# A state-space layer with an MLP on one core: the written-out order of 1078 operations is searched anew

## The chip, the core and the metric

One core of a Trainium2 chip. The metric is device microseconds for one execution of the whole program; the kernel before and the kernel after are run on the same kind of core and compared. In the profile the engines are called PE (TensorE, matmuls; PEld its weight loads), DVE (VectorE), ACT (ScalarE), POOL (GpSimd) and SP (SyncE, which here only issues DMAs).

## The reference

The input u has 2048 steps of 512 channels (bf16). It is normalized, sent through a diagonal state-space layer (a long convolution whose kernel K is built from 128 complex exponentials for each channel), added to itself, normalized twice more, and sent through an MLP with 1376 hidden units. Cut to what matters:

```python
def _A_ref(u, A_re, A_im, B_re, B_im, C_re, C_im, log_dt, Dskip):
    dt = jnp.exp(log_dt)[:, None]
    logdA, dB = dt * (A_re + 1j * A_im), dt * (B_re + 1j * B_im)
    l = jnp.arange(L).astype(A_re.dtype)                     # bf16
    P = jnp.exp(logdA[:, :, None] * l[None, None, :])
    K = jnp.einsum("dn,dnl,dn->dl", C_re + 1j * C_im, P, dB).real
    ...                                                      # both padded to 2 L
    Yf = rfft2(up) * rfft2(Kp)
    y = irfft2(Yf)[..., :L]
    return y.transpose(0, 2, 1) + u * Dskip

def _B_ref(x, w1, b1, w2, b2):
    h = gelu(einsum("bsd,df->bsf", layernorm(x), w1) + b1)
    return einsum("bsf,fd->bsd", h, w2) + b2

h = x + _A_ref(layernorm(x), ...)
return h + _B_ref(layernorm(h), w1, b1, w2, b2)
```

## The kernel before

The program first makes a list of 1078 operations, each with the engines that it may run on, a cost for each, and what it reads and writes. Then `Sched.run` walks through `ORDER`, a list written out by hand: a value k stands for operation `k // 2`, and `k % 2` picks the first or the second of its allowed engines. A cost is used for three things only: a planned start of each operation, the merging of the engines by that start, and the placing of fills. On one engine the operations are issued in the order of the list, so costs alone do not reorder an engine. The core of it:

```python
for k in ORDER:
    i, e = k // 2, ops[k // 2].eng[k % 2]
    s = max(free[e], ready(ops[i], e), ...)
    ...
    if e == "PE" and s > FILL0 and s - free[e] > 0.6 and fs:
        ...   # dummy matmuls of 512 columns up to s, through Sched.fill (line 1443)
order.sort(key=lambda o: (o.start, o.i))
```

A fill is such a dummy matmul: it stands on PE where the plan sees PE waiting for over 0.6 us, and its result is not used. Matmul results go to four PSUM buffers of 128x1024 floats. An eviction copies such a buffer to the arena in SBUF (the tile `ar`), on ScalarE (line 554) or VectorE (line 556) as the list says. Most DMAs go through SP's queue, in the order of the list; log_dt, C_re and B_re are issued by ScalarE, ahead of its work. The convolution is done as a two-step Fourier transform of 64 by 32 points, with the matrices of cosines and sines made on the chip. The stages, with the names that the prediction uses:

- *Loads and tables.* The parameters are transposed on PE. dt is an Exp (ScalarE). The angles of A_im are wrapped and restacked by 16 small DMAs on SP. GpSimd makes constants, among them the weights W2 for the chains (line 718) and a mask block: `R_fn` (lines 842 to 846) and its product with a one-hot row (a TT, line 612). From these it makes the masks W of the frequency matrices (line 602).
- *Statistics and normalizing of u.* Sixteen bn_stats (line 906) and, later, sixteen normalizing steps (line 915) on VectorE.
- *Exponentials.* `bexps` (line 767) are sixteen Exp steps on ScalarE; `aexps` (matmuls at 983, 987) five for each half of the channels.
- *Chains.* `chain(half, kind)` builds the powers of the complex exponentials, as B0, A0, B1 and A1. For each group of four powers PE adds a phase in PSUM (line 1029), ScalarE takes two sines (line 1037) and VectorE multiplies (lines 1055 to 1057, for A1 1042 and 1043).
- *Transforms of u.* `austage` (line 928) regroups u into AU_d in DRAM, X0 and X1 are read back by SP, and `xspec`/`fstage` (line 954) transforms them. X0 and X1 are the two halves of the sequence.
- *Kernel chunks.* `kgen` (lines 1079, 1080; chunks 0 and 1) and `kgen4` (1110, 1111; chunks 2 and 3) contract the powers over the 128 states. After each chunk one VectorE step (line 1093, or 1120) adds Dskip to its first tap; the prediction calls it the correction. `kspec` (line 1144) is the first step of the chunks' transform; its result makes a round trip through AK_d in DRAM, and `fstage` does the second step.
- *Inverses.* `inverse(b, c)` for half b and chunk c: products of spectra on VectorE (line 1184), 96 or 192 small matmuls (line 1194), an eviction, and on SP a transposing DMA (the "transpose" of an inverse, line 1200).
- *Tails.* `tail(b, sb)`: matmuls (line 1274) that put the halves together and, for the first tail, add u; bn_stats and, but for the first, an addition ahead of it (lines 1281, 1282); a Newton iteration of small VectorE steps for the inverse root; four normalizing steps (VectorE at 1297 or ScalarE at 1299); and a transpose, on PE for the first tail (line 1307), by DMA for the others. The Gelu table is loaded once, on ScalarE.
- *MLP.* `mlp(b, sb)` four times: matmuls at line 1328, Gelu on ScalarE (1330), matmuls at line 1350, an addition on VectorE (1352), two DMAs out.

Of the kernel before, what the change touches and what calls it, by code (L numbers as in the profile page):

```python
# [154 lines left out]
class VS(V):  # L155
# [260 lines left out]
def c_act(n, ptr=0):  # L416
    return 0.055 + n / 1200.0 + 0.09 * min(ptr, 1)
# [7 lines left out]
def kernel(ctx, tc, A_u, A_A_re, A_A_im, A_B_re, A_B_im, A_C_re, A_C_im, A_log_dt, A_Dskip,  # L425
# [125 lines left out]
    def evac(out_fn, in_fn, n, r, w, pr=None, only=None):  # L551
# [5 lines left out]
        if only == "ACT":  # L557
            add("ACT", c_act(n), fn, r=r, w=w, pr=pr)
        elif only == "DVE":
            add("DVE", c_dve(n, 1, True), fn, r=r, w=w, pr=pr, hv=0)  # L560
        else:
            add(("ACT", "DVE"), (c_act(n), c_dve(n, 1, True)), fn, r=r, w=w, pr=pr)
# [925 lines left out]
```

## Time and profile before

| | |
|---|---|
| three runs | 262.06, 262.65 and 264.29 us, median 262.65 |
| the profiled execution | 262.22 us, its span 260.4 us, mean granted clock of TensorE 0.991 |
| busy in the span | PE 226.0 us (87%), VectorE 185.7 (71%), ScalarE 172.0 (66%), GpSimd 50.2 (19%) |
| DMA | 34.34 MB, mean 132 GB/s |
| ScalarE's table of sines loaded | 37.26 to 38.54 us |
| first chain product, last A0 product, last A1 product | 51.7, 74.8, 105.3 us |
| first matmul of line 1144 | 95.9 us |
| first matmul of inverse (1,0) | 131.5 us |
| end of the last product of inverse (0,3) | 153.96 us |
| first matmul of the first tail, first matmul of the MLP | 161.6, 174.2 us |
| last matmul | 256.6 us |

The span runs from the first to the last recorded instruction; the 1.8 us to the execution's own time lie around it. The points in time in the lower half are how the prediction cuts the kernel into stages: each is the start or the end of a named group of instructions in the trace. A busy share of PE is not work alone, since fills count as matmuls (line 1443).

### The profile page before, as it was taken

The numbers are of one execution on the slowest core, as the hardware profiler recorded it, in microseconds if no ns is written. First come the engines' busy times: TensorE is split into PE (matmuls) and PEld (weight loads), VectorE is DVE, ScalarE is ACT, GpSimd is POOL, SyncE is SP. The second block draws the span as 40 slices with busy tenths as digits, with TensorE's granted clock in tenths as the row PEclk, the third lists the DMA queues.
The fourth block names the chain that finished last, engine by engine and source line by source line (L and its number), as shares of the span: only waits on it lengthen the run. The fifth ranks groups of instructions, "written<-read, shape, count | busy, mean of one in ns | idle before, by whom it ended". The sixth has DMA issues, their size and how long they took to land.

```text
span 260.4 us, 7255 instructions
## 1 busy us (share of the span) xinstructions
PE 226.0 (87%) x3019; PEld 130.7 (50%) x3032; DVE 185.7 (71%) x363; ACT 172.0 (66%) x207; POOL 50.2 (19%) x236
## 2 busy tenths in 40 slices
PE   7209995868698988999999999799999999989994
PEld 3105751423475654675578885464344444434542
DVE  3999999999998889666899996798585424021021
ACT  3989997958997569768996970757602913912710
POOL 8934442997028000000000000000000000000000
PEclk9999999997999999999999999999999999999999
DMA  6600011463584458679289899999341402050303
GB/s 203 262 0 3 3 45 35 124 117 89 121 279 130 128 149 297 219 215 331 90 239 255 227 179 200 265 168 252 81 85 25 94 7 49 18 99 23 88 5 76
DMA packets 46001, 34.34 MB, mean 132 GB/s; under 512 B 26161, under 2 KB 42386, under 8 KB 45970
## 3 DMA queue, kind: packets, MB, share of 16 engines
q1 hardware_dynamic: 45378, 33.44, 48.6%
q10 hardware_dynamic: 592, 0.46, 0.6%
q8 instruction: 23, 0.38, 0.6%
q14 instruction: 8, 0.07, 0.1%
HBM read 16.32 MB, written 10.49 MB: 103 GB/s over the span
## 4 chain that ended last, share of the span: by engine, by line
PE 59%; DVE 23%; ACT 8%; DMA 4%; issue 4%; POOL 0%; DVEq 0%; ACTq 0%; POOLq 0%
PE ps L1328 13%; PE ps L1350 13%; PE ps L1194 7%; PE ps L954 4%; DMA ar<-ar 4%; ACT ar L554 4%; PE ps L1144 4%; DVE ar L906 3%; PE ps L1029 3%; ACT ar L1037 3%; DVE ar L915 3%; DVE ar L1056 3%; DVE ar L612 3%; DVE ar L617 2%; PE ps L1274 2%
## 5 line engine op out<-in xcount | busy, mean ns | idle before, releaser
L554 ACT CAST ar<-ps 128x1024 bf16<-128x1024 f32 (+3 forms) x69 | 63.2, 983 | 20.2 <-DVE ar L1282 6.9
L1330 ACT ACTIVATE ar<-ps,ar 128x512 bf16<-128x512 f32 (+1 forms) x44 | 28.7, 686 | 40.4 <-PE ps L1328 27.0
L1352 DVE TENSOR_TENSOR ar<-ps,ar 128x512 bf16<-128x512 f32 (+1 forms) x17 | 11.0, 658 | 45.0 <-PE ps L1350 43.1
L1328 PE MATMUL ps<-ar 128*128 128x512 bf16 (+1 forms) x176 | 40.3, 379 | 1.0 <-DMA ar<-ar 0.7
L1037 ACT ACTIVATE ar<-ps 128x1024 bf16<-128x1024 int16 x36 | 34.9, 1044 | 8.0 <-DVE ar L1056 3.2
L1350 PE MATMUL ps<-ar 128*128 128x512 bf16 (+3 forms) x181 | 39.7, 366 | 0.3
L556 DVE CAST ar<-ps 128x1024 bf16<-128x1024 f32 (+4 forms) x31 | 32.7, 1070 | 8.0 <-PE ps L1111 3.6
L602 POOL TENSOR_SCALAR ar<-ar 128x128 bf16<-128x128 bf16 (+6 forms) x60 | 31.0, 540 | 18.6 <-ACT ar L624 18.1
L1184 DVE TENSOR_TENSOR ar<-ar 128x1024 bf16<-128x1024 bf16 x48 | 30.1, 685 | 3.3 <-PE ps L1194 2.0
L1328 PEld LDWEIGHTS <-ar 128*128 128x128 bf16 (+1 forms) x176 | 17.5, 100 | 22.2 <-issue 2.6
L1350 PEld LDWEIGHTS <-ar 128*128 128x128 bf16 (+1 forms) x187 | 18.1, 98 | 20.5 <-issue 1.1
L1029 PE MATMUL ps<-ar 128*32 128x256 f16 x560 | 22.0, 279 | 4.9 <-ACT ar L1037 4.4
L1194 PE MATMUL ps<-ar 64*128 64x128 bf16 x768 | 23.5, 216 | 1.8 <-DVE ar L1282 1.4
L1194 PEld LDWEIGHTS <-ar 64*128 64x128 bf16 x768 | 21.6, 94 | 5.3 <-issue 2.8
L1029 PEld LDWEIGHTS <-ar 128*32 128x32 f16 x560 | 13.8, 97 | 14.4 <-issue 14.1
L954 PE MATMUL ps<-ar 128*64 128x512 bf16 (+1 forms) x160 | 17.8, 342 | 0.7 <-DVE ar L556 0.4
L767 ACT ACTIVATE ar<-ar 128x1024 bf16<-128x1024 f32 x16 | 15.9, 1047 | 1.1 <-DVE ar L600 1.1
L1056 DVE TENSOR_TENSOR ar<-ar 128x1024 bf16<-128x1024 bf16 x21 | 16.1, 783 | 0.2
L983 PE MATMUL ps<-ar 128*128 128x512 f16 x24 | 7.4, 430 | 9.8 <-DVE ar L600 9.6
L1057 DVE TENSOR_TENSOR ar<-ar 128x1024 bf16<-128x1024 bf16 x21 | 14.0, 690 | 0.3
L624 ACT ACTIVATE ar<-ar 128x512 f32<-128x512 f32 (+8 forms) x18 | 11.7, 679 | 3.6 <-DMA ar<-in_A_log_dt_dram 2.7
L928 PE MATMUL ps<-ar 128*128 128x512 bf16 x26 | 8.7, 411 | 5.2 <-DVE ar L600 4.0
(99 smaller groups left out, 315.2 us busy)
## 6 DMA issues: line engine op xcount, KB each, us to landing
AU_d<-ar SPq DMA_DIRECT2D x16, 256.0 KB, 3.8
ar<-AU_d SPq DMA_DIRECT2D x8, 512.0 KB, 4.1
ar<-AK_d SPq DMA_DIRECT2D x8, 512.0 KB, 5.9
ar<-in_A_u_dram SPq DMA_DIRECT2D x4, 512.0 KB, 5.3
AK_d<-ar SPq DMA_DIRECT2D x2, 1024.0 KB, 4.4
ar<-in_A_u_dram SPq DMA_DIRECT2D x8, 256.0 KB, 4.7
AK_d<-ar SPq DMA_DIRECT2D x4, 512.0 KB, 3.6
out_dram<-ar SPq DMA_DIRECT2D x30, 64.0 KB, 2.0
```

What stands on the lines that cost most here:

```text
L554: act.copy(out_fn(), in_fn())
L556: dve.tensor_copy(out_fn(), in_fn())
L602: en.tensor_scalar(a, b, f(s1), f(s2), op0, op1)
L954: pe.matmul(pst(p)[64 * h:64 * h + 64, w * (k + r):w * (k + r) + w], lhsT=T.ap()[:, f, r, :], rhs=v[f:f + 1].ap()[:, 0, :], start=True, st ...
L1029: pe.matmul(pst(p)[32 * g:32 * g + 32, 256 * j:256 * j + 256], lhsT=W2[DELTAS.index(d)].ap(), rhs=S2[g].ap()[:, ch0:ch0 + 256], start=Fals ...
L1037: add("ACT", c_act(1024), lambda e, p=p, sc=sc, cs=cs: act.activation(swo(sc[cs]) if hf and kind == "B" else sc[cs].ap().rearrange("p a b ...
L1056: add("DVE", c_dve(1024, 2), lambda e, lo=lo, rv=rv, Sx=Sx, e0=e0, i0=i0, q=q: dve.tensor_tensor(ent(i0, q, lo, 4, rv), ent(e0, q, lo, 4, ...
L1184: dve.tensor_tensor(o, a, b_[:, :, ::-1, :] if sw else b_, ALU.mult)
L1194: pe.matmul(pst(p)[:, 512 * h + 128 * k:512 * h + 128 * k + 128], lhsT=q.ap()[rows, 2 * k + r, :], rhs=TP[w].ap()[rows, f0 // 2 + k, :], s ...
L1328: pe.matmul(pst(p)[:fs, 512 * z:512 * z + 512], lhsT=w1s[dc].ap()[:, fc * P:fc * P + fs], rhs=ybuf.ap().rearrange("p (t c) k -> p c t k", ...
L1330: add("ACT", c_act(512, 1), lambda e, p=p, z=z, fc=fc, fs=fs: act.activation(hT.ap()[:fs, fc, :], pst(p)[:fs, 512 * z:512 * z + 512], ACT. ...
L1350: pe.matmul(pst(p)[:, 512 * z + c0:512 * z + c1], lhsT=hT.ap()[:fs, fc, 128 * t:128 * t + 128], rhs=w2s[fc].ap()[:fs, c0:c1], start=(fc == ...
```

## The change

The computation, the buffers, the operations and the tiles stay as they are, and so do all line numbers. Two things are edited. The list `ORDER` is another permutation of the same 1078 operations, with another choice of engine for some; and the costs that the planner uses are changed for evictions, products, normalizing of u and most kinds of matmuls. Cut to its core (46 lines of numbers are replaced):

```diff
 ORDER = [
-    22, 28, 24, 82, 0, 358, 60, 30, 2, 4, 8, 114, 288, 112, 90, 188, 190, 32, 118, 6, 78, 72, 116, 122, 156, 134, 26, 286, 34, 36, 38, 272, 158, 160, 68,
...
+    288, 358, 306, 0, 4, 362, 24, 114, 2, 68, 8, 30, 76, 32, 34, 36, 38, 72, 22, 112, 156, 188, 190, 118, 116, 122, 128, 78, 152, 158, 26, 54, 64, 6, 120,
...
 ]
     def evac(...):
-            add("ACT", c_act(n), fn, r=r, w=w, pr=pr)
+            add("ACT", c_act(n) + (0.1 if n > 700 else 0), fn, r=r, w=w, pr=pr)
     def unorm(pr):
-            add("DVE", c_dve(512, 4) + 0.13, ufn, ...)
+            add("DVE", c_dve(512, 4) + 0.23, ufn, ...)
     def fstage(v, nb, soft=()):
-            add("PE", 0.86 if nb == 1 else 0.45, fn, ...)
+            add("PE", 0.99 if nb == 1 else 0.53, fn, ...)
     def aexps(pr):
-                add("PE", 1.75 if n < 3 else 0.88, fn, ...)
+                add("PE", 1.93 if n < 3 else 0.97, fn, ...)
     def chain(hf, kind, pr):
-                o = add("PE", 0.55 + (0 if gn else 0.45 if kind == "B" else 1.3), fn, ...)
+                o = add("PE", 0.58 + (0 if gn else 0.47 if kind == "B" else 1.36), fn, ...)
-                add("DVE", c_dve(1024, 2), ...)              # each of the four products
+                add("DVE", c_dve(1024, 2) + 0.08, ...)
     def kgen(c, pr):
-                    add("PE", 0.14 * (hi - lo), fn, ...)
+                    add("PE", 0.148 * (hi - lo), fn, ...)
     def kgen4(c, pr):
-                add("PE", 0.13 * h, fn, ...)
+                add("PE", 0.148 * h, fn, ...)
     def kspec(b, q, pr, ak, nb, n):
-                add("PE", 4 * len(vs) * (0.22 if par is None else 0.12), mm, ...)
+                add("PE", 4 * len(vs) * (0.255 if par is None else 0.14), mm, ...)
     def inverse(b, c, pairs, zt, pr):
-            add("PE", 0.47 * len(jobs), fn, ...)
+            add("PE", 0.479 * len(jobs), fn, ...)
     def tail(b, sb, ybuf, pr):
-            add("PE", 0.85 if first else 0.43 * (1 + b), fn, ...)
+            add("PE", 0.98 if first else 0.5 * (1 + b), fn, ...)
-                add("PE", 0.3, fn, ...)                      # transposes
+                add("PE", 0.33, fn, ...)
```

What the new list does, read from the order in which each engine is given its instructions:

- *Engines.* Of 104 evictions 72 were on ScalarE and 32 on VectorE; now 77 and 27. Of the tails' sixteen normalizing steps eight were on each; now ten are on ScalarE.
- *Fills* go from 49 to 38, and stand elsewhere: before, 16 behind the exponentials of A, 3 in chain B1, the rest beside the inverses (15 around inverse (1,2), 12 in inverse (1,3)); now 15 behind the exponentials, 11 beside inverse (1,2), 6 in inverse (1,3), and a few single ones.
- *DMA issues.* ScalarE issues C_re ahead of log_dt; SP issues A_im behind all four loads of u; SP's loads of w1 and x stand elsewhere between the transposes.
- *GpSimd.* The mask block and the constants of u's transform move behind the product for the angle of A (the TT of `gi`); W2 stays ahead of the chains.
- *PE.* The transforms of X0, which stood among the sines of A1, move for the most part behind the kernel chunks; the first half of inverse (1,0) goes ahead of inverse (0,0).
- *First tail.* Its small statistics steps, which had four products of an inverse between them, stand together; the Gelu table is loaded between its evictions.

More of the change, by code (lines that the diff above doesn't have):

```diff
@@ L561, in evac @@
         else:
-            add(("ACT", "DVE"), (c_act(n), c_dve(n, 1, True)), fn, r=r, w=w, pr=pr)
+            add(("ACT", "DVE"), (c_act(n) + (0.1 if n > 700 else 0), c_dve(n, 1, True)), fn, r=r, w=w, pr=pr)
     def dma(q, out_fn, in_fn, byts, r, w, pr=None, soft=(), k=1.0):
@@ L915, in ufn @@
                 dve.tensor_scalar(a, a, sc_, bi_, ALU.mult, ALU.add)
-            add("DVE", c_dve(512, 4) + 0.13, ufn, r=[x_sb[s], nw[3], nw[4]], w=[x_sb[s]], pr=pr + 0.001 * (s // 4))
+            add("DVE", c_dve(512, 4) + 0.23, ufn, r=[x_sb[s], nw[3], nw[4]], w=[x_sb[s]], pr=pr + 0.001 * (s // 4))
     def austage(b, pr, soft=()):
@@ L988, in aexps @@
                 S.pr = pr + 0.1 * n + 0.5 * hf
-                add("PE", 1.75 if n < 3 else 0.88, fn, r=[HLt] + [WA[LV.index(LD[4 * n + j])] for j in range(4)] + ([HLg, Ih] if n < 3 else []), w=[p], new=[p] if n < 3 else [], soft=[TBL])
+                add("PE", 1.93 if n < 3 else 0.97, fn, r=[HLt] + [WA[LV.index(LD[4 * n + j])] for j in range(4)] + ([HLg, Ih] if n < 3 else []), w=[p], new=[p] if n < 3 else [], soft=[TBL])
                 if hf == 0:
@@ L1080, in fn @@
                                 pe.matmul(o, lhsT=Ai.ap()[:, :, d], rhs=Bi.ap()[:, :, d], start=False, stop=True, tile_position=(0, 32 * g))
-                    add("PE", 0.14 * (hi - lo), fn, r=[Ar, Br, Ai, Bi], w=[p], new=[p] if first else [])
+                    add("PE", 0.148 * (hi - lo), fn, r=[Ar, Br, Ai, Bi], w=[p], new=[p] if first else [])
                     first = False
@@ L1111, in fn @@
                         pe.matmul(o, lhsT=w(Ai), rhs=x(Bi), start=False, stop=True)
-                add("PE", 0.13 * h, fn, r=[EA2, Br, IA2, Bi], w=[p], new=[p] if b == 0 else [])
+                add("PE", 0.148 * h, fn, r=[EA2, Br, IA2, Bi], w=[p], new=[p] if b == 0 else [])
             def ofn(j0=j0, h=h):
@@ L1144, in mm @@
                             pe.matmul(oo, lhsT=W[v].ap()[rows, tl, :], rhs=r, start=(m == 0), stop=(m == len(js) - 1), tile_position=(32 * g, 0))
-                add("PE", 4 * len(vs) * (0.22 if par is None else 0.12), mm, r=[kg, W], w=ps, new=ps if first else [])
+                add("PE", 4 * len(vs) * (0.255 if par is None else 0.14), mm, r=[kg, W], w=ps, new=ps if first else [])
                 first = False
@@ L1274, in fn @@
                             pe.matmul(o[64 * h:64 * h + 64], lhsT=DD.ap()[:, di].rearrange("p a b -> p (a b)"), rhs=rhs, start=(n == 0 and not first), stop=(n == len(terms) - 1))
-            add("PE", 0.85 if first else 0.43 * (1 + b), fn, r=[identb, DD] + [hs[8 * b + 4 * sb + 2 * jp + z] for z in range(2)] + ZT0 + (ZT1 if b else []), w=[p], new=[p])
+            add("PE", 0.98 if first else 0.5 * (1 + b), fn, r=[identb, DD] + [hs[8 * b + 4 * sb + 2 * jp + z] for z in range(2)] + ZT0 + (ZT1 if b else []), w=[p], new=[p])
             for z in range(2):
```

16 lines of the change are left out of this document (8 added, 8 removed), and 78 rows, old and new, of the table ORDER.

## The prediction

> **What bounds the kernel now.** I read the page, then the busy times in six stages that I cut at the starts of groups of matmuls, then the chain that ended last, then the groups by shape. The first two lines are the page, the others the stages: after the span come PE, weight loads, VectorE, ScalarE and GpSimd busy, the granted clock, the DMA share and GB/s.
>
> ```profile
> span 260.4 us, 7255 instructions
> ...
> PE 226.0 (87%) x3019; PEld 130.7 (50%) x3032; DVE 185.7 (71%) x363; ACT 172.0 (66%) x207; POOL 50.2 (19%) x236
> ...
> 41.60:75.00 33.40, 25.78 (x382) 12.56 (x391) 32.60 (x58) 28.16 (x31) 17.35 (x32) 0.95 0.49 124
> 75.00:104.00 29.00, 26.20 (x829) 17.74 (x833) 26.11 (x41) 22.08 (x26) 7.18 (x14) 1.00 0.57 183
> 104.00:131.50 27.50, 26.74 (x354) 17.16 (x344) 19.76 (x26) 23.15 (x26) 0.52 (x1) 1.00 0.66 213
> 131.50:157.60 26.10, 25.28 (x686) 21.09 (x686) 25.36 (x38) 20.60 (x22) 0.00 (x0) 1.00 0.92 228
> 157.60:174.20 16.60, 14.64 (x248) 9.24 (x249) 11.79 (x33) 7.17 (x10) 0.00 (x0) 1.00 1.10 213
> 174.20:256.60 82.40, 81.05 (x392) 37.18 (x396) 32.90 (x90) 34.95 (x53) 0.00 (x0) 1.00 0.31 71
> ```
>
> From 41.6 to 75 (chains B0 and A0) VectorE is full, 32.60 of 33.40, and PE waits. From 75 to 104 PE and VectorE are both near full. From 104 to 131.5 PE is. From 131.5 to 157.6 (the inverses) VectorE is full again, 25.36 of 26.10; PE's 25.28 holds fills. The last row, the MLP, is PE alone: 81.05 of 82.40. The row ahead of it is not work but a chain of latencies:
>
> ```profile
> 151.80 2.81 PE ps L1194 x96
> 154.68 0.86 ACT ar L554
> 155.59 1.03 ACT ar L554
> 156.63 4.96 DMA ar<-ar
> 161.63 0.41 PE ps L1274 x2
> ...
> 172.51 1.08 PE ps L1307 x16
> 173.61 1.02 ACT ar L554
> 174.68 7.93 PE ps L1328 x36
> ```
>
> The evictions of inverse (0,3) end, their transposing DMA takes 4.96 us, the tail's first matmul starts at once, and 13 us of statistics, normalizing and transposes follow until the MLP. So the run's end is the MLP's start plus some 82 us of matmuls.
>
> **The change, part by part.** Nothing is computed otherwise; 1078 operations stand in another order, and some move between ScalarE and VectorE. For both kernels I took the order of issue on each engine and summed, ahead of chosen instructions, the durations of the same form in this trace (for matmul groups, from the start of one to the start of the next). The sums differ from elapsed time by some per cent, as instructions overlap at their ends or wait, so I use differences, scaled by what the same stretch took before. The forms that move:
>
> ```profile
> L554 ACT CAST ar<-ps 128x1024 bf16<-128x1024 f32 x61 | 58.7, 1026 | 10.3 <-PE ps L1194 3.8 <-PE ps L954 3.1 <-PE ps L928 1.5
> L556 DVE CAST ar<-ps 128x1024 bf16<-128x1024 f32 x19 | 23.0, 1218 | 2.6 <-PE ps L954 1.7 <-PE ps L928 0.7
> L1299 ACT ACTIVATE ar<-ar 128x512 bf16<-128x512 bf16 x8 | 6.3, 807 | 3.5 <-DVE ar L617 3.5
> L1297 DVE TENSOR_SCALAR ar<-ar 128x512 bf16<-128x512 bf16 x8 | 3.0, 411 | 0.1
> ```
>
> *Engines.* Evictions on VectorE fall from 32 to 27 and rise on ScalarE from 72 to 77; normalizing steps go from 8 and 8 to 6 on VectorE and 10 on ScalarE. The net five are small: six of 264 to 792 columns leave VectorE, one more of 1024 comes to it. In sums VectorE loses 4.4 us and ScalarE gains 4.9. Fills fall from 49 to 38; at 0.216 us from start to start 11 are 2.4 us, but they stand where PE waited, so I don't add them.
>
> *To the start of L1144, 95.9: +0.1.* On ScalarE's queue log_dt is now issued behind C_re, 0.43 us later (issues stood at 0.77 and 1.20), and ScalarE, with 36.4 us of work ahead of its sine table in both, passes that on; but VectorE sets this stretch from 34 us. Its work up to the correction of the kernel's second chunk (L1093), the last step ahead of L1144, is 91.5 in both. In between it is moved: up to the last A0 product 2.0 us more (two evictions and a B1 product go ahead), from there 1.8 less. PE has 0.2 more ahead of L1144. Bounds: -1.3, the part of VectorE's work in 75 to 95.9 that would be saved if the A0 products weren't waited for (1.8, less 0.5); +4.7 by ScalarE, which has 4.3 us more ahead of the last eviction that L1144 needs, plus the 0.4. ScalarE idled 12.2 us in 41.6 to 104, so I take VectorE's value. A_im now follows all four loads of u on SP; its first user on VectorE stood at 21.97 us, 12 us after its transpose, and PE had nothing else until 19.5: free. GpSimd's mask block (L842 2.62 us, L612 2.16) moves behind the product for the angle; W2, which the first chain needs, still comes ahead of the restacked angles, which land at 44: free, up to 5 us; what it may do to VectorE is a rival.
>
> *95.9 to 131.5 (first matmul of inverse (1,0)): 0.* PE is full and has 29.1 us of work in both. VectorE's last A1 product comes 4.0 us of work sooner and the AK_d DMAs some 2 us sooner after L1144, but the X0 transforms (L954), which stood among the A1 sines, now stand here and PE does not finish earlier. Bounds: -2.6, PE's three longest gaps of 79 to 99 us (0.92, 0.93, 0.74); 0.
>
> *131.5 to the last product of inverse (0,3), 153.9: -0.8.* VectorE decides. Before, it ends the last eviction that the inverses need at 132.5 and has 22.9 us of work to that product, done in 21.4. After, the like eviction ends just as inverse (1,0) starts (+0.1), and 23.0 follow: 21.5. So 21.6 against 22.4. Bounds: -2.3, PE's count (19.8 to 17.5); 0. On SP, ahead of the transpose of (0,3), one 344 KB load of w1 is added and one 256 KB load of x goes: free.
>
> *From there to the MLP: -0.9.* The 4.96 us transpose stays. From the tail's first matmul to the MLP it was 13.4 us. Now the 15 small statistics steps stand together instead of with four 0.68 us products among them, but three normalizing steps are on ScalarE at 0.81 instead of 0.41, and the Gelu table (1.28) is loaded inside. Step by step: 1.5 to the first bn_stats, 4.0 for four of them and two products, 2.8 statistics, 2.4 normalizing, 0.3 transposes, 1.5 eviction and start: 12.5. Bounds: -2.4, the 11 fills with their waits; +1.3, the table load in full.
>
> *MLP: -0.7.* Same matmuls. Its one stall is 0.73 us at 231.8, for the transpose of the last tail, whose matmuls now stand 4.7 us of PE work sooner. The one ahead of it is issued later, behind the first MLP's output sums, with some 20 us of matmuls to cover it; without that cover, 4.7.
>
> Sum: 0.1 - 0.8 - 0.9 - 0.7 = -2.3. The profiled run took 262.2 (span 260.4 and 1.8 around it), 0.4 below the median of 262.65. Forecast **259.9**.
>
> **The rivals.**
> *ScalarE sets the pace (slower).* If its waits stay as they are, the work moved to it comes on top: +4.7 at L1144, the inverses -0.8, the tail +1.3 with the table load in full, the MLP -0.7: 266.7. For: ScalarE ran 81% from 41.6 to 104. Against: part of its idle time is VectorE's buffers, which come sooner:
>
> ```profile
> ACT ar L1037 <- DVE ar L1056: 3.2, 3, 2.0
> ```
>
> It decides once ScalarE is above some 95% there.
> *GpSimd holds VectorE up (slower).* Two L915 steps, 0.41 us each elsewhere, took 2.40 together while GpSimd ran two steps of 1.29:
>
> ```profile
> 38.41 2.40 DVE L915 TENSOR_SCALAR ar<-ar 128x512 bf16<-128x512 bf16 x2
> ```
>
> Such losses after 27 us were 1.6 here and 1.5 at one L602 (1.96 instead of 0.43). The moved block and what follows it last 2.62 + 2.16 + 1.19 + 1.29 + 1.29 = 8.6 us, now beside VectorE's sixteen L915. If all of it held VectorE, 8.6 - 3.1 = 5.5 more: 265.4. Against: the nine bn_stats (L906) beside two GpSimd steps at 24 us kept their 0.68 us each, so not every kind is held. [...]
> *The DMA hides it (no change).* The share is 0.92 and 1.10 ahead of the MLP. If the transposes land when they did, only tail and MLP are left: 260.7; if each engine waits for its producers as before, 262.2. Against: the transposes wait on SP for evictions.
> *More gain*, the full bounds of inverses, tail and MLP: 262.2 - 2.3 - 2.4 - 0.7 = 256.8, and with the gaps 254.2.
>
> **How the numbers follow.** Forecast 0.38 (its own range 257.8 to 261.5), more gain 0.18, no change 0.16, GpSimd 0.08, ScalarE 0.20. Run times differ by 0.9% here, so 1% is about what can be told. Below 260.0: more gain and 0.24 of the forecast's 0.38, as its own range reaches further below than above, 0.42. Above 265.3: ScalarE, and some of GpSimd's, 0.22. Within: 0.36. The range runs from 255.0, short of the fullest gain, to 266.7, ScalarE's price.
>
> **What would show it.** Right: the first L1144 within 1 us of 95.9, the first matmul of inverse (1,0) near 131.5, the MLP's first L1328 near 172.6, 27 evictions on VectorE, no stall in the MLP. Wrong: ScalarE above 95% from 41.6 to 104 with a late L1144; L915 above its mean of 0.51 us; a transpose of over 6 us ahead of the tail; an MLP of over 82.4 us. An L1144 ahead of 94 would show that counting VectorE's work misses waits that the list takes away.

## The result, and the profile after

The change made the kernel slower: 265.64 us (median of 20 executions, 262.84 to 267.50) against 263.74 us (20 executions, 262.06 to 266.76), a ratio of 1.0065 with a 95% interval of 1.0038 to 1.0092. The forecast was 259.9, which is 2.8 below the 262.65 that three executions of before gave; against all twenty the change is +1.9 by medians and +1.8 by means. Ratios with intervals leave out executions over 1.5% above the fastest of their kernel, which favours a kernel that scatters; medians and means are over all. `ORDER` holds 1079 operations, numbered 0 to 1078, so one more than the 1078 named above. The profiled execution of the kernel after took 265.12 us. The page:

```profile
span 263.3 us, 7270 instructions
...
PE 227.4 (86%) x3021; PEld 131.7 (50%) x3021; DVE 183.9 (70%) x356; ACT 176.9 (67%) x214; POOL 56.5 (21%) x236
...
PEclk9999979998999999999999999889999999999998
```

VectorE lost work and ScalarE gained it, as forecast, and PE has the same work. VectorE's busy time fell by 1.8 us only, not by the 4.4 that were counted; the steps that were held, below, fill the gap. What is new is GpSimd, 56.5 us busy instead of 50.2 for the same 236 instructions, and two more dips of PE's clock. The cut at the times used before shows that GpSimd's time was added from 41.6 to 75, where its mask steps (L602, 128x128) stand; columns as before:

```profile
41.60:75.00 33.40, 26.25 (x381) 12.37 (x381) 32.91 (x66) 29.40 (x34) 24.08 (x36) 0.95 0.49 129
75.00:104.00 29.00, 24.35 (x801) 17.09 (x793) 21.68 (x38) 23.08 (x28) 5.20 (x11) 1.00 0.50 153
...
157.60:174.20 16.60, 14.52 (x225) 9.22 (x221) 10.46 (x29) 9.28 (x12) 0.00 (x0) 0.90 1.08 195
174.20:256.60 82.40, 81.59 (x461) 37.95 (x458) 34.98 (x95) 37.15 (x56) 0.00 (x0) 1.00 0.36 77
```

The 24.08 us of GpSimd in the first row are not the loss: the first experiment below has 24.48 there and loses nothing. These rows have shifted against the work, so I cut both kernels again at the starts and ends of the same operations (us; the last column has two other profiles of the old order: the mask block later in the kernel before, and the old list with the new costs):

| stretch | before | after | old order again |
|---|---|---|---|
| to the first L928 | 41.6 | 44.7 | 41.6, 41.7 |
| to the first chain product (L1056) | 51.7 | 55.3 | 51.8, 51.8 |
| from there to the first matmul of inverse (1,0) | 79.8 | 78.9 | 80.2, 81.2 |
| to the last product of inverse (0,3) | 22.5 | 21.9 | 22.6, 22.9 |
| to the tail's first matmul that did not wait | 7.7 | 8.2 | 7.7, 7.7 |
| to the MLP's first that did not wait | 13.3 | 14.9 | 14.8, 14.8 |
| the MLP | 81.7 | 80.3 | 81.6, 80.8 |

The kernel after is 3.6 us late before the first product of the chains, gets 1.5 us back up to the inverses' last product, loses 2.1 around the tail and gains 1.4 in the MLP: 2.8 in all. The profile of before that I predicted from was a good one of its kind: its tail had the full clock and took 13.3 us, where the same order took 14.8 twice, at a clock of 0.88. A fourth profile of that order (codT and product elsewhere, below) had the full clock and 13.3 again.

### The profile page after: what moved, and what is told of

Its sections match the earlier page's. It is cut to its first block, busy times and chain, and to the rows that moved or that the text cites. A ratio compares the mean times of both kernels' runs of the same rounds, so it can differ in the third digit from the quotient of the medians.

```text
span 263.3 us, 7270 instructions
## 1 busy us (share of the span) xinstructions
PE 227.4 (86%) x3021; PEld 131.7 (50%) x3021; DVE 183.9 (70%) x356; ACT 176.9 (67%) x214; POOL 56.5 (21%) x236
## 4 chain that ended last, share of the span: by engine, by line
PE 56%; DVE 25%; ACT 9%; issue 5%; DMA 4%; ACTq 0%; DVEq 0%
PE ps L1328 15%; PE ps L1350 15%; PE ps L1194 6%; PE ps L954 5%; DVE ar L617 4%; ACT ar L1037 3%; DVE ar L906 3%; ACT ar L554 3%; PE ps L1144 3%; DVE ar L600 3%; DVE ar L612 3%; DVE ar L1056 2%; DMA ar<-ar 2%; PE ps L1029 2%; DVE ar L1057 2%
## 5 line engine op out<-in xcount | busy, mean ns | idle before, releaser
L554 ACT CAST ar<-ps 128x1024 bf16<-128x1024 f32 (+3 forms) x74 | 66.4, 959 | 18.8 <-PE ps L1274 5.2
L602 POOL TENSOR_SCALAR ar<-ar 128x128 bf16<-128x128 bf16 (+6 forms) x60 | 37.3, 642 | 9.4 <-DVE ar L602 7.9
L556 DVE CAST ar<-ps 128x1024 bf16<-128x1024 f32 (+3 forms) x26 | 29.2, 1140 | 9.6 <-PE ps L1111 3.1
L1184 DVE TENSOR_TENSOR ar<-ar 128x1024 bf16<-128x1024 bf16 x48 | 29.9, 685 | 5.5 <-PE ps L1194 5.4
L1328 PEld LDWEIGHTS <-ar 128*128 128x128 bf16 (+1 forms) x176 | 17.3, 100 | 20.7 <-issue 1.0
L1194 PE MATMUL ps<-ar 64*128 64x128 bf16 x768 | 25.2, 222 | 1.9 <-issue 1.3
L1194 PEld LDWEIGHTS <-ar 64*128 64x128 bf16 x768 | 22.9, 97 | 5.6 <-issue 4.1
L1029 PE MATMUL ps<-ar 128*32 128x256 f16 x560 | 20.9, 276 | 3.3 <-issue 1.9
L1029 PEld LDWEIGHTS <-ar 128*32 128x32 f16 x560 | 13.9, 97 | 11.9 <-issue 11.6
L954 PE MATMUL ps<-ar 128*64 128x512 bf16 (+1 forms) x160 | 17.0, 341 | 0.4 <-ACT ar L554 0.3
L983 PE MATMUL ps<-ar 128*128 128x512 f16 x24 | 8.0, 454 | 8.6 <-DVE ar L600 5.7
L617 DVE SCALAR_TENSOR_TENSOR ar<-ar 128x4 f32<-128x4 f32 (+5 forms) x44 | 14.4, 335 | 1.2 <-ACT ar L624 0.3
L1056 DVE TENSOR_TENSOR ar<-ar 128x1024 bf16<-128x1024 bf16 x21 | 14.4, 707 | 0.8 <-ACT ar L1037 0.7
L1057 DVE TENSOR_TENSOR ar<-ar 128x1024 bf16<-128x1024 bf16 x21 | 14.3, 716 | 0.3 <-ACT ar L1037 0.2
```

The costliest lines, as they stand in the source:

```text
L554: act.copy(out_fn(), in_fn())
L556: dve.tensor_copy(out_fn(), in_fn())
L602: en.tensor_scalar(a, b, f(s1), f(s2), op0, op1)
L617: add("DVE", c_dve(n, 1, psum), lambda e: dve.scalar_tensor_tensor(oap() if oap else o.ap(), aap() if aap else a.ap(), f(s), bap() if bap ...
L954: pe.matmul(pst(p)[64 * h:64 * h + 64, w * (k + r):w * (k + r) + w], lhsT=T.ap()[:, f, r, :], rhs=v[f:f + 1].ap()[:, 0, :], start=True, st ...
L1029: pe.matmul(pst(p)[32 * g:32 * g + 32, 256 * j:256 * j + 256], lhsT=W2[DELTAS.index(d)].ap(), rhs=S2[g].ap()[:, ch0:ch0 + 256], start=Fals ...
```

## What holds VectorE ahead of the chains

The answer to the first two rows lies at 28 to 38 us of the kernel after. The timeline of GpSimd, then of VectorE (start, us, instruction, shapes, count):

```profile
28.62 0.87 POOL L842 MEMSET ar<- 128x928 f32 x1
29.54 1.50 POOL L846 MEMSET ar<- 128x1 f32 x44
...
31.32 2.20 POOL L612 TENSOR_TENSOR ar<-ar 128x928 f32<-128x928 f32 x1
33.46 0.31 POOL L679 MEMSET ar<- 128x256 bf16 x1
33.76 3.64 POOL L602 TENSOR_SCALAR ar<-ar 128x1024 int32<-128x1024 int32 x2
```

```profile
29.81 1.70 DVE L602 TENSOR_SCALAR ar<-ar 128x512 f32<-128x512 f32 x1
31.44 2.11 DVE L617 SCALAR_TENSOR_TENSOR ar<-ar 128x16 f32<-128x16 f32 x1
33.47 0.68 DVE L612 TENSOR_TENSOR ar<-ar 128x512 f32<-128x512 f32 x1
34.07 1.74 DVE L600 TENSOR_SCALAR ar<-ar 128x512 f16<-128x512 f32 x3
35.73 2.21 DVE L617 SCALAR_TENSOR_TENSOR ar<-ar 128x16 f32<-128x16 f32 x3
37.86 1.35 DVE L915 TENSOR_SCALAR ar<-ar 128x512 bf16<-128x512 bf16 x1
```

A step of 16 columns, 0.16 us elsewhere, took 2.11 us: it began 0.12 us after the mask block's product on GpSimd and ended as that did. ScalarE's next step, the Ln of u's statistics, waited 2.4 us for it:

```profile
33.58 0.56 ACT L624 ACTIVATE ar<-ar 128x16 f32<-128x16 f32 x2 [2.43 <-DVE ar L617]
```

From the held step on, the chain that ended last runs through these VectorE steps to the first L928, and through no GpSimd step; so it was not a result of GpSimd that came late:

```profile
31.52 2.03 DVE ar L617
...
34.15 1.67 DVE ar L600 x3
35.81 2.12 DVE ar L617 x3
37.94 2.89 DVE ar L915 x6
...
44.68 2.46 PE ps L928 x10
```

The L602 beside the memsets, and one step in each group beside the two codT steps, were stretched in the same way. Summed over all VectorE instructions that start between 10 and 45 us (duration less the shortest of the same operation in any profile, where that is over 0.3 us), the held time is 5.9 us; in the kernel before it is 3.2, of which the same product has 1.55, on an L602:

```profile
27.90 1.96 DVE L602 TENSOR_SCALAR ar<-ar 128x512 f32<-128x512 f32 x1
```

My theory after the result: this held time made the front late, and the rest of the new list is about as good as forecast. The rivals: that the new order on ScalarE and VectorE itself is late in the front; that the new costs, by their fills, are the loss; and that the rest of the list is no better.

## Experiments on the hold

**Four GpSimd steps issued earlier** (order of the kernel after, only GpSimd's changed):

```diff
   ... L602 (identity weights, to 12 us)
+  L842 to L850 (mask block), L612 (its product), L602 x2 (codT)
   L612 (HLg) ... L612 (product for the angle) ... L602, L857
-  L842 to L850 (mask block)
   L857
-  L612 (its product)
   L679
-  L602 x2 (codT)
   L696, L718 (W2)
```

> The kernel after, with four GpSimd steps issued earlier: the mask block (L842), its product with the one-hot row (L612) and the two steps for codT (L602) go ahead of GpSimd's subtraction for HLg, into the stretch near 12 us where GpSimd was idle. Nothing else is moved. GpSimd theory: in the kernel after these four ran at 28.6 to 37.4 us and held VectorE's small steps (L617 2.11 us instead of 0.17, L600 1.09, L617 1.52, L915 1.35), 2.8 us more than before between 20 and 44 us; so the first L928 comes back from 44.7 to about 41.9 and the time is some 2.8 us below the kernel after, 0.997 of before. Rival (ScalarE's or VectorE's own order in the new list makes the front late): the first L928 stays within 0.5 us of 44.7, and the ratio to before stays at 1.0065. If the four steps hold VectorE just as much near 12 us, the loss moves there and L928 stays late too, with long VectorE steps at 12 to 20 us.

Measured: 262.27 us (median of 12) against 263.40 for before in the same session, ratio 0.9924 (0.9889 to 0.9960), by medians 0.996. First L928 at 42.5, first chain product at 52.5. The moved steps held one VectorE step at 15 us, an L612 (the second of these two; one of 0.68 took 2.63):

```profile
14.38 3.23 DVE L612 TENSOR_TENSOR ar<-ar 128x512 f32<-128x512 f32 x2
```

```profile
14.57 2.50 POOL L612 TENSOR_TENSOR ar<-ar 128x928 f32<-128x928 f32 x1
17.06 3.23 POOL L602 TENSOR_SCALAR ar<-ar 128x1024 int32<-128x1024 int32 x2
```

Held time fell from 5.9 to 3.0, the first product came 2.8 us sooner, and the whole loss was gone, with 1.1 us more. ScalarE's order was untouched and its table of sines still ended at 41.4 (41.8 after), so its lateness is not what set the front.

**Only the codT steps earlier:**

```diff
   ... L602 (identity weights, to 12 us)
+  L602 x2 (codT)
   ...
   L857, L612 (mask block's product), L679
-  L602 x2 (codT)
```

> The kernel after, with only the two codT steps (L602, 128x1024) issued early on GpSimd; the mask block and its product stay behind the angle's product, at 28 to 33 us. In the kernel after, the two codT steps held VectorE steps (L600 by 0.9, L617 by 0.85, L915 by 0.95 us), the product one small L617 by 1.95 and the memsets one L602 by 1.3. Theory A (all held time counts alike, and the product costs some 2 us wherever it stands, so that what the first experiment won came from the codT steps and the memsets): first L928 about 2.3 us ahead of the kernel after, at 42.4, ratio to before near 0.996. Theory B (what hurt was the product falling on the small statistics step that ScalarE waited 2.43 us for): L928 stays past 44, ratio near 1.005.

Measured: 264.38 against 263.56, ratio 0.9999 (0.9969 to 1.0030), by medians 1.003; held 4.2 us, first L928 at 43.4, first chain product at 54.0. It lies between the two theories: the codT steps account for about 1.3 us, the mask block and its product for the other 1.5 (54.0 to 52.5).

**The mask block later in the kernel before:**

```diff
-  L842 to L850 (mask block)                 # at 7.2 us
   ...
+  L842 to L850 (mask block)                 # at 27.0 us
   L612 (its product)
```

> The kernel before with one GpSimd step moved: the making of the mask block (L842, 2.62 us) goes from 7.2 us to just ahead of its product, so that the product (L612, 2.16 us) falls on 30 to 32 us, where VectorE does the small statistics of u that ScalarE's Ln waits for. GpSimd theory: one of those steps of 0.17 us is held for about 2 us, ScalarE waits for it, and the first L928 goes from 41.6 to some 43.3; the time rises by 1.5 to 2, ratio 1.006 to 1.008. Rival (GpSimd does not matter, the new list's order on ScalarE and VectorE does): within 0.3 us of before.

Measured: 263.27 against 263.40, ratio 0.9992 (0.9962 to 1.0022). My expectation failed, and why is of use: the product at 29.7 us did hold a step, an L600 that took 2.26 us, but where it had stood before it had held one too, an L602 that took 1.96. At both places there was one step to hold. The first L928 stayed at 41.6.

**The product twice** (kernel after, nothing moved):

```diff
-    TT(R, R, oh, ALU.mult, ..., eng=("POOL", "DVE"))
+    def two_fn(e):
+        for _ in range(2):
+            gp.tensor_tensor(R.ap(), R.ap(), oh..., ALU.mult)
+    add("POOL", 2 * (0.12 + 928 / 480.0), two_fn, ...)
```

> The kernel after with the mask block's product done twice on GpSimd, one behind the other (the one-hot row is 0 or 1, so the block stays the same); nothing else is changed. GpSimd theory: VectorE, which was held 1.95 us by the one product, is held by some 2 us more near 33 us; the first L928 goes from 44.7 to some 46.7 and the first chain product from 55.3 to 57; the time rises by 1 to 2 us, ratio to before 1.011 to 1.015. Rival (the held step is not on the path): L928 within 0.5 us of 44.7, ratio 1.007.

Measured: 267.91 against 263.94, ratio 1.0132 (1.0086 to 1.0178), 2.3 us above the kernel after by medians. A second VectorE step was held, an L600 for 2.61 us (in the group of three of the third line); the first L928 came at 47.4 and the first chain product at 57.5:

```profile
31.98 2.11 DVE L617 SCALAR_TENSOR_TENSOR ar<-ar 128x16 f32<-128x16 f32 x1
34.01 0.68 DVE L612 TENSOR_TENSOR ar<-ar 128x512 f32<-128x512 f32 x1
34.61 3.96 DVE L600 TENSOR_SCALAR ar<-ar 128x512 f16<-128x512 f32 x3
```

**The product on VectorE** (on the kernel with four steps early):

```diff
-  GpSimd:   L612 128x928 behind L850
+  VectorE:  L612 128x928 behind L602 (wrap of the angle), near 30 us
```

> The kernel of the first experiment (four GpSimd steps early), with the mask block's product (L612) on VectorE instead of GpSimd, near 30 us. In the first and second experiments that product held one VectorE step for as long as it ran, wherever it stood: 2.63 us instead of 0.68, and 2.26 instead of 0.42. GpSimd theory: done by VectorE itself it takes about 1.0 us (928 columns at the rate of the L612 of 512 columns in 0.68 us would be 1.2), so VectorE saves 0.8 to 1.0 us ahead of the first L928 (42.5 to 41.6), and the time is 0.5 to 1 us below the first experiment. Rival (a VectorE step held at 15 us is not on the path, since VectorE waits for ScalarE or loads around it): VectorE only gets 1.2 us of work more, and L928 comes 1 us later than in the first experiment.

Measured: 262.65 against 263.56, ratio 0.9944 (0.9916 to 0.9973). VectorE did the product in 1.20 us where it had been held for 1.95; the first L928 came at 41.6 as the theory said. The time did not follow: it is the same as with the four steps early, within their intervals.

**The codT steps and the product elsewhere in the kernel before:**

```diff
+  L602 x2 (codT)                            # idle stretch from 14 us
   L1374, L679, L857, L602
   L612 (HLg)
-  L602 (codT)
+  L612 (mask block's product)               # beside bn_stats
   ...
-  L612 (mask block's product)
   ...
-  L602 (codT)
```

> The kernel before with three GpSimd steps moved: the two codT steps (L602) into the idle stretch of GpSimd near 15 us, the mask block's product (L612) behind the product for HLg, at about 25 us, beside bn_stats (L906) alone, which no GpSimd step has held in any profile. GpSimd theory: VectorE loses 1.5 us less at its L602 near 28 us and 1.7 us less at its two L915 near 38 us; the first L928 goes from 41.6 to about 39, the first chain product from 51.7 to about 50, and the time falls by 1 to 2.5 us, ratio 0.990 to 0.996. Rival (in the old list ScalarE's chain to the table of sines, which ends at 38.5, sets the first chain product): L928 earlier, first chain product within 0.5 us of 51.7, ratio 1.000.

Measured: 264.09 against 264.05, ratio 0.9994 (0.9963 to 1.0024). The product itself, beside nine bn_stats, held nothing, but the hold moved: the codT steps now held an L617 (1.49 us, 0.69 in the kernel before) and an L602 (1.09, 0.23 before) at 16 to 18 us, and two L915 at 38 to 40 us (2.73 together, 2.40 before) were held as before, by the GpSimd steps that moved up to there (the product for the angle, L612, and W2, L718); these four make up the held time of 3.7, which was 3.2. So it does not tell what the old list would win.

**The product beside bn_stats** (on the kernel with the readers of the tail sorted, below):

```diff
-  L612 (mask block's product) behind L850   # 14.6 us
   L612 (HLg), six L602, L857
+  L612 (mask block's product)               # 24.2 us
   L612 (product for the angle)
```

> The kernel with four GpSimd steps early and the readers of the first tail sorted, with the mask block's product moved from 14.6 us to behind GpSimd's identity weights, at about 24 us, where VectorE does bn_stats (L906) but for one step. GpSimd theory: at 14.6 us the product held a VectorE L612 with two inputs from SBUF for 1.95 us; beside bn_stats it holds nothing, so VectorE gains up to 1.9 us ahead of the first L928 (41.8 to 40 or 40.5) and the time falls by 0.5 to 1.5 us, to some 260.5, ratio 0.987. Rival (as when the product went to VectorE: what is won ahead of L928 is absorbed in the chains): L928 earlier by over 1 us, ratio as before it, 0.991 within 0.3%.

Measured: 261.20 (median of 6, 257.43 to 262.61) against 264.05, ratio 0.9774 (0.9720 to 0.9827, from three executions); by medians 0.989. First L928 at 40.4, first chain product at 50.5. GpSimd and VectorE in that stretch:

```profile
24.16 2.15 POOL L612 TENSOR_TENSOR ar<-ar 128x928 f32<-128x928 f32 x1
```

```profile
21.41 4.24 DVE L906 BATCH_NORM_STATS2 ar<-ar 128x6 f32<-128x512 bf16 x7
25.56 0.67 DVE L617 SCALAR_TENSOR_TENSOR ar<-ps,ar 128x512 f32<-128x512 bf16 x1
26.15 1.87 DVE L906 BATCH_NORM_STATS2 ar<-ar 128x6 f32<-128x512 bf16 x3
```

The product ran for 2.15 us, and nothing beside it was stretched: the bn_stats kept a start every 0.6 us, and so did an L617 that takes one of its inputs from PSUM. The front came 1.4 us sooner than with the readers sorted alone (50.5, 51.9), so the hold depends on what VectorE does meanwhile. It is the fastest kernel here, but its time is not told apart from that one's: -3.3 us with a standard error of 0.8, and -1.8 with 0.6.

All that bears on the hold in one table (held: as defined above; time against before of the same session, by means, with its standard error):

| kernel | held, us | first chain product | time, us |
|---|---|---|---|
| product beside bn_stats | 1.4 | 50.5 | -3.3 (0.8) |
| product on VectorE | 1.5, and 1.2 of its own | 51.7 | -1.3 (0.4) |
| four steps early | 3.0 | 52.5 | -0.9 (0.5) |
| four steps early, readers of the tail sorted | 3.1 | 51.9 | -1.8 (0.6) |
| all of it together | 1.6, and 1.2 of its own | 51.9 | +1.4 (0.6) |
| before | 3.2 | 51.7 | 0 |
| before, three steps moved | 3.7 | 52.1 | +0.1 (0.4) |
| before, mask block later | 4.1 | 51.8 | -0.2 (0.3) |
| codT early only | 4.2 | 54.0 | +0.8 (0.5) |
| after | 5.9 | 55.3 | +1.8 (0.4) |
| after, with the old costs | 5.9 | 55.2 | +4.2 (0.9) |
| after, product twice | 8.1 | 57.5 | +4.3 (0.6) |

In the kernels with the new list the first product goes with the held time (and the 1.2 us), from 1.4 to 8.1 us, by about one to one. The time does so too, but for two kernels: all of it together, and the new list with the old costs. Their chains begin as early as the held time says, so what they lose, they lose elsewhere (below).

The held steps and the free ones differ in part by their inputs: of the steps with two inputs from SBUF the L617 of 16 columns took 2.11 us and an L612 of 512 took 2.63, while the bn_stats and the L617 with one input from PSUM kept their 0.6 to 0.7. But steps of one input were held too, an L600 (2.26) and an L602 (1.96). What decides which step is held was not shown.

## Experiments on the rest of the list

The four mixed orders that come first all have the new costs, which alone make the old list 1.0 us slower (further down); a gain of that size in the rest of the list could hide behind it.

**The order of before up to the first L1144, then the new one:**

```diff
-ORDER = new
+ORDER = old[:position of the first L1144] + what is left, in the new order
```

> The order of the kernel before up to the first L1144, then the order of the kernel after for all that is left. In the profiles the two lists took 95.9 and 101.0 us to the first L1144, then 35.6 and 33.1 to the first matmul of inverse (1,0). Theory of separate stages: the new list is worse by 5.1 ahead of L1144 and better by 2.5 behind it; then here L1144 starts near 95.9, inverse (1,0) near 129.0, and the time is below before by 2 us, ratio 0.992. Rival (what came late at L1144 was caught up because VectorE, ScalarE and the DMAs of the next stretch were not late): inverse (1,0) near 131.5 again, ratio 1.000 within 0.3%.

Measured: 262.89 against 263.40, ratio 1.0001 (0.9970 to 1.0033). The first L1144 came at 100.8, as in the kernel after, though everything ahead of it had the old order: the cut left it behind three groups of A1's sine matmuls, where the new list has it. Inverse (1,0) began at 132.9 all the same, 81.2 us after the first chain product, as in the old list with the new costs. So a first L1144 that is 5 us late does not delay the inverses, and its 5.1 us say nothing of the loss.

**The order of before up to the first L928, then the new one:**

```diff
+ORDER = old[:position of the first L928] + what is left, in the new order
```

> The order of the kernel before up to the first L928 (regrouping of u), then the order of the kernel after for all that is left. Theory (what the new list loses is lost ahead of the first L928 and is GpSimd's; the rest of the list is better than the old one, as forecast): first L928 at 41.6 and first chain product at 51.7 as before, the time 1 to 2 us below before like the kernels with the GpSimd steps early (262.4 in the mean), ratio 0.992 to 0.996. Rival (the rest of the new list is no better, and the early GpSimd steps won something of their own): ratio 1.000, within 0.3%.

Measured: 264.42 against 263.94, ratio 0.9979 (0.9938 to 1.0020), by medians 1.002, executions from 261.49 to 267.75. L928 came at 41.8, but the first chain product at 53.1, so the seam cost 1.4 us of its own. This does not decide whether the rest of the list is better.

**The new order up to the first tail, then the old one:**

```diff
+ORDER = new[:position of the first tail's matmuls] + what is left, in the old order
```

> The order of the kernel after up to the first matmul of the first tail, then that of the kernel before. In the profiles it is 13.1 us from the tail's first matmul that did not wait to the MLP's first before, and 14.6 after; the MLP's matmuls took 82.1 and 80.3. Theory (the new list makes the tail longer, since evictions and bn_stats of one PSUM buffer alternate with the table load in between and three normalizing steps stand on ScalarE, and makes the MLP shorter): tail 13.1, MLP 82.1, the sum 0.3 longer than after, ratio to before 1.007. Rival (the MLP's difference is not in the list): tail 13.1, MLP 80.3, ratio 1.001.

Measured: 266.47 (median of 6) against 263.40, ratio 1.0136 (1.0084 to 1.0189). The tail took 15.2 us, not 13.1, and the MLP 81.6. Behind the new order the old list's tail is no better.

**The old order up to the first tail, then the new one:**

```diff
+ORDER = old[:position of the first tail's matmuls] + what is left, in the new order
```

> The order of the kernel before up to the first matmul of the first tail, then that of the kernel after. It is the counterpart of the kernel that took the old order from the tail on, whose MLP took 81.6 us against 80.3. Theory (the forecast's last two steps): MLP 80.3, tail 14.7 at most, as in the other profiles of the new order, so 1.2 us of the MLP and nothing of the tail are won: ratio 0.995. By the forecast's own numbers (tail -0.9, MLP -0.7) 0.994. Rival (what is won in the MLP is lost in the tail): 1.000 to 1.005.

Measured: 267.84 (median of 6) against 263.94, ratio 1.0130 (1.0083 to 1.0176). The expectation failed, and the kernel is among the slowest: the MLP took its 80.3 us, but the tail 17.3, with a clock of 0.90. The MLP's 80.3 thus belongs to the new list; ten other profiles with the new order there show it too (all of it together, below, has 83.6). A tail's length depends on what stands ahead of it (the new list's took 14.9 in the kernel after); why this one is the longest was not separated, so neither mixed order tells what one list's tail is worth alone.

**The old list with the new costs, and the new list with the old costs** (only the fills move):

> The list of the kernel before with the planner's costs of the kernel after: every engine has its instructions in the old order, and only the fills stand elsewhere (52 instead of 49, seven of them single pairs in the chains). Theory (costs alone do nothing, as fills stand where PE waits): within 0.4% of before, and the profile is a second look at the old order: first L928 at 41.6, inverse (1,0) near 131.5, from the tail's first matmul to the MLP 13.1 us, the MLP 81.6. Rival (part of the loss comes from fewer or displaced fills, by the granted clock): a changed ratio of over 0.5%.

> The list of the kernel after with the planner's costs of the kernel before: every engine has its instructions in the new order, and only the fills stand elsewhere (37 instead of 38; none behind inverse (1,3)'s first half, two behind inverse (0,3)'s). The new costs on the old list had cost 1.0 us in the mean, 0.4%. Theory (that was the seven fills put into the chains of the old list; the new list has none there with either set of costs): the time stays that of the kernel after, ratio 1.006 within 0.4%, first L928 at 44.7, first chain product at 55.3. Rival (the new costs cost 0.4% whatever the list): ratio 1.002 to 1.003.

Measured: 264.59 against 263.56, ratio 1.0037 (1.0006 to 1.0069); and 268.23 (median of 6) against 264.05, ratio 1.0121 (1.0074 to 1.0168), by medians 1.016. Each list is slower with the costs of the other, the new one by 2.6 us in the medians. So the new costs are not the loss; with the new list they win. Of the expectations the first held for the time, though the tail took 14.8 us and not 13.1; the second failed. So it matters where the fills stand. In the new list with old costs, with two fills in the tail instead of eight, the granted clock from the tail to the MLP (16.2 us) was 0.79, where it was 0.89 in the kernel after:

```profile
169.00:185.20 16.20, 12.41 (x167) 8.65 (x167) 13.41 (x36) 9.55 (x13) 0.00 (x0) 0.79 1.07 213
```

```profile
164.20:179.10 14.90, 12.18 (x173) 7.80 (x173) 12.03 (x33) 9.67 (x13) 0.00 (x0) 0.89 1.08 210
```

The first row is from the slowest of that kernel's six executions (271.48 us). How much of the 2.6 us the clock accounts for was not separated.

**The readers of the first tail's PSUM buffers, sorted** (on the kernel with four steps early):

```diff
-  ScalarE:  evict 0b, table, evict 0a, 1a, 1b      VectorE:  stats 0a, product, 0b, product, 1a, 1b
+  ScalarE:  evict 1a, 1b, 0b, 0a ... table         VectorE:  stats 0a, 0b, two products, 1a, 1b
```

> The kernel of the first experiment, with the readers of the first tail's two PSUM buffers in another order: VectorE takes both bn_stats of the first buffer while ScalarE takes both evictions of the second, then the other way round; and the Gelu table is loaded behind the last eviction on ScalarE ahead of the MLP, where ScalarE waits for PE. Before, readers of one buffer on the two engines waited for each other in turn (the list alternates them, with the table load between two), 5.7 us from the first eviction to the end of the fourth bn_stats in the kernel after. Theory (this chain of alternating readers is what made the tail 14.6 instead of 13.1 us): that stretch takes about 3.8 us, the tail 12.7, and the time is 1.5 to 2 us below the first experiment, 260.5, ratio 0.989. Rival (the tail is paced by something else, PE's inverse (1,3) or the normalizing steps): under 0.5 us.

Measured: 261.51 (median of 6) against 263.56, ratio 0.9907 (0.9871 to 0.9942); 0.8 us below the four steps early, half of what was expected and within both intervals. From the tail's first matmul to the last bn_stats it took 4.85 us instead of 6.8, as expected; but the tail as a whole 14.5 instead of 14.9. The 2 us went to two places: ScalarE's normalizing steps stood behind an eviction that waited for matmuls that took longer (inverse (1,3), 2.96 us for 64 instead of 1.96), and the other 64 of that inverse still stand ahead of the MLP.

**All of it together:**

```diff
+  VectorE:  normalizing 2a, 2b, 1b; ScalarE: 1a, eviction of inverse (1,3) behind them
+  PE:       second half of inverse (1,3) behind the MLP's first two groups
+  VectorE:  the mask block's product
```

> The kernel with the readers of the first tail's PSUM buffers sorted, with three more edits: the mask block's product on VectorE (as in the kernel that tried that alone), three of the first tail's four normalizing steps on VectorE (0.41 us instead of 0.81) with ScalarE's eviction of inverse (1,3) behind them, and on PE the second half of inverse (1,3) behind the MLP's first two groups instead of ahead of them. Theory (the tail is a chain from bn_stats over the normalizing steps to the transposes, and PE has other work to fill it with): tail 12.5 to 13 us instead of 14.5, time 260 to 260.5, ratio 0.985 to 0.988. Rival (PE's own work, at a lower granted clock in the tail, sets the MLP's start): within 0.3% of the kernel with the readers sorted, 0.991.

Measured: 265.93 (median of 12) against 263.94, ratio 0.9992 (0.9944 to 1.0039), by medians 1.008. The profiled execution, the shortest of the twelve, had a tail of 11.6 us, shorter than expected, and an MLP of 83.6: together 95.2, as in the kernel after. The chain in the tail:

```profile
165.81 6.11 DMA ar<-in_B_w_dram
171.92 0.04 issue
171.96 1.71 PE ps L1328 x7
173.67 0.00 issue
173.68 1.98 PE ps L1194 x64
```

With the tail shortened, the MLP waits for a load of w1, and the matmuls that were taken out of the tail stand in the MLP. Why most executions are some 4 us longer than the profiled one stays open.

## Why the prediction was wrong, step by step

*The step that failed* is the sentence on GpSimd in the step to the first L1144: the mask block "moves behind the product for the angle ... free, up to 5 us; what it may do to VectorE is a rival". It was put into the sum at nothing and given a chance of 0.08. With the codT steps, which the new list moved too, it cost 2.7 us of held VectorE time, which is three quarters of the 3.6 us by which the chains began late (where the other 0.9 went stays open); undone alone, it took the whole loss away. The rival had the hold and the stretch right, not the steps, and its 5.5 was twice the size; that its 265.4 met the median is an accident of the sum. I had measured the hold (2.40 us at two L915), but looked for more of it at L915 only. L915's mean went down, from 0.51 to 0.46 us. Most of the steps that were held were others, among them one of 16 columns, and with it ScalarE. The held L602 of before (1.96 us instead of 0.43) had shown that L915 is not the only form; counting every step beside the moved GpSimd steps, the bn_stats left out, would have taken the others in.

*L1144 within 1 us of 95.9* was a bad marker: it came 5.1 us late, and the experiment with the old order up to it shows that it can do so at no cost to the inverses. The step behind it, forecast at 0, came out at -2.5 for the same reason; the two should have been one term.

*ScalarE sets the pace*, the slower rival I gave most, did not happen: from 41.6 to 75 ScalarE was busy 29.40 of 33.40 us, 88%, and the four early GpSimd steps won without a change on ScalarE.

*The inverses, -0.8*: right; -0.6 in the profile (22.5 to 21.9).

*The transpose of 4.96 us stays*: it took 5.89 in this profile:

```profile
158.25 5.89 DMA ar<-ar
164.19 0.41 PE ps L1274 x2
...
165.29 0.59 ACT ar L554
165.91 0.70 DVE ar L1282
...
167.84 1.08 ACT ar L554 x2
168.95 0.71 DVE ar L1282
169.69 0.59 ACT ar L554
170.31 0.71 DVE ar L1282
...
173.76 2.22 ACT ar L1299 x3
175.98 0.90 ACT ar L554
176.93 1.96 PE ps L1194 x64
178.89 7.90 PE ps L1328 x36
```

*Tail, -0.9*: wrong in sign. The clock is not the reason: the kernel with the product twice has the new tail at the full clock, and it took 14.9 us as well:

```profile
169.90:184.80 14.90, 10.71 (x173) 6.59 (x173) 12.26 (x33) 9.51 (x13) 0.00 (x0) 1.00 1.04 213
```

Against the old order at a clock of 0.88 (14.8) nothing is lost; against its 13.3 at the full clock, 1.6. The chain shows two terms that were missed. ScalarE's evictions and VectorE's bn_stats of one PSUM buffer took turns, in the order of the list, so the four bn_stats took 5.1 us and not 4.0: L1282 waited 2.2 us for L554 in three places, and L554 1.4 us for L1282 in two. And the second 64 matmuls of inverse (1,3), which before ran in a gap of the tail, stand ahead of the MLP: 2.4 us from the transposes to the MLP, not 1.5.

*MLP, -0.7*: right in sign, twice the size (81.7 to 80.3; PE's two waits there, 0.73 us at 231.8 and 0.17 at 204, are gone). But tail and MLP should have been one term. From the tail's first matmul to the last of the MLP it was 94.9 before and 95.2 after, and 95.2 with a tail 3.3 us shorter: what PE did not do in that tail, it did in the MLP.

*Engines* came as counted:

```profile
L554 ACT CAST ar<-ps 128x1024 bf16<-128x1024 f32 x60 | 57.6, 1024 | 10.1 <-PE ps L954 4.7 <-PE ps L1194 4.5 <-PE ps L1144 0.6
...
L1299 ACT ACTIVATE ar<-ar 128x512 bf16<-128x512 bf16 x10 | 7.8, 804 | 3.8 <-DVE ar L617 3.8
...
L1297 DVE TENSOR_SCALAR ar<-ar 128x512 bf16<-128x512 bf16 x6 | 2.4, 406 | 0.0
```

With the hold undone or on VectorE, the new list is 0.9 to 1.3 us better than the old one by means (standard errors 0.5 and 0.4), about half of the 2.3 forecast.

## What to carry to other kernels

When a list or a scheduler moves a GpSimd step, it is not enough that its result comes in time: look at which VectorE steps stand beside its new place, and whether they are of a form that was held here: L617 and L612 with two inputs in SBUF (2.11 us and 2.63), L600 (2.26), L602 (1.96), L915 (two in 2.40). The smallest of them, of 0.16 us, was held to the end of a GpSimd step of 2.20, and ScalarE, which waited for it, stood for 2.43. A place beside bn_stats was free here, twice (a start every 0.6 us in the fastest kernel), and so was one beside a step that reads one of its inputs from PSUM (0.67 us). Cut stages at events that lie on the path, and put two neighbouring stages into one term if the same engine can move work between them.

## What the runs showed of the hardware that was not expected

A GpSimd step of 2.2 us held a VectorE step of 0.16 us until its own end, and doubling it held another for 2.61. Beside memsets of 1 and 4 columns on GpSimd an L602 of one input took 1.70 us instead of 0.41. And the same order of instructions, with the same 13 fills, had a granted clock of 1.00 in the tail of two profiles and of 0.88 in that of a third, 13.3 against 14.8 us:

```profile
161.60:174.90 13.30, 11.47 (x177) 6.98 (x179) 10.23 (x30) 7.85 (x11) 0.00 (x0) 1.00 1.06 217
```

```profile
162.30:177.00 14.70, 13.16 (x177) 8.35 (x178) 10.15 (x30) 7.92 (x11) 0.00 (x0) 0.88 0.94 195
```

The first is the kernel before, the second that with the mask block later. A term of a sum taken from one profile carries this with it. What made the difference was not shown.
